# Sink keys in the own key block: query blocks of 112 in a fused attention and gated FFN kernel

## The chip, the cores and the metric

The kernel runs on one core of a Trainium2 chip. The metric is the device time of one execution in microseconds (us). The core has a matrix engine (TensorE, PE in the profile; its weight loads are shown apart as PEld), two engines for elementwise work (VectorE, DVE, and ScalarE, ACT), GpSimd (POOL), which here issues most of the loads, and SyncE (SP), whose queue carries a few loads, the transposing transfers and the stores. Matrix products accumulate in PSUM; everything else is held in the on-chip memory SBUF.

## The reference

What is computed is an attention with a sliding window and sinks, and then a feed-forward part without a nonlinearity. There are 4 batches, 8 heads, 768 tokens and 64 dimensions a head. A query sees the 128 keys up to and including its own, and the first 4 keys of the sequence, the sinks.

```python
scores = scale * np.matmul(q, k.transpose(0, 1, 3, 2))
rel = pos[:, None] - pos[None, :]
keep = (pos[None, :] < 4) | ((rel >= 0) & (rel < 128))
a = softmax(np.where(keep, scores, -1e9))
attn = np.matmul(a, v)
x = attn.transpose(0, 2, 1, 3).reshape(3072, 512)
out = ((x @ w1) * (x @ w2)) @ w3 @ w_out
```

w1 and w2 are 512 by 1024, w3 is 1024 by 1024, w_out is 1024 by 512. The output is 3072 by 512 in float32.

## The kernel before

**Folding.** The product w3 @ w_out does not depend on the tokens, so the kernel makes it once (`w3o`): TensorE transposes w3 in halves of a row block (`fold_w3`, tasks "t3", tile `w3t`, line 407) and multiplies pieces of it with w_out (`fold_mm`, "fm", tiles `ph` and `pw`, line 437). Each token then needs two gate products and one projection.

**Attention.** Keys and queries of a block of 128 tokens arrive as rows (`kN`, `qN`) and are turned into `kqT`, in which a head's 64 dimensions lie across partitions. For batches 0 and 1 TensorE does that (`transposes`, "tpk", tile `tp`, line 213), for batches 2 and 3 a transposing transfer on SP's queue ("tdk", "tdq", line 220). Values (`vN`) stay as they arrive, with a column of ones that gives the softmax its sum. Scores are made with keys across partitions (`scores`, "sc", line 260; batch 0's first blocks through `block_scores`, line 281): one call is for one pair of heads and one unit of 256 queries, two blocks, each with the block of keys before it and its own. ScalarE takes exponentials (`ex`), VectorE multiplies a 0/1 mask (`am`), and `values` ("av", line 350) loads each 128 by 128 piece of `am` as weights and streams the 65 columns of values and ones. VectorE divides by the sum (`rec`, `xn`).

**Sinks.** The 4 sink keys lie outside most windows. `sink_keys` ("sk", line 228) copies them into `ksbd`, which has 32 columns of weights for each pair of heads; `sink_scores` ("ss", tile `sp`, line 242) multiplies them with the queries after the first 256, for four pairs at once, and `es` is their exponential. `sink_values` ("sv", line 233) lays out the sink values (`vs`). In `values`, each block after the first unit starts with a product of `es` and `vs` that is 130 columns wide, both heads in one.

**FFN.** The normalized output is transposed to `xT`, by TensorE ("xt") for batch 0 and by transfers on SP's queue ("xd") for the others. `gate` ("g", line 390) makes one of the two gate products for 128 of the 1024 hidden columns and one stretch of tokens (`CHUNKS`): 3 x 256 tokens in batches 0 and 1, 2 x 384 in batches 2 and 3. ScalarE copies the first half (`a_sb`), VectorE multiplies the second with it into `ab`. `project` ("p", tile `po`, line 451) multiplies `ab` with `w3o`, and ScalarE (for one piece VectorE) copies the result out for a store.

**What sets the order.** Every step is a task. `plan()` simulates the engines with a table of costs, and picks at each moment the task that starts first and, among those, has the best priority; `nudge` shifts the priority of four tasks. The order so found is emitted, one in-order stream for each engine, so at run time an engine that waits for one operand holds everything behind it. PSUM holds four "mm" buffers for all but scores ("ph" apart) and two larger ones for scores. GpSimd's queue carries the loads in the order of the list `order`; an issue waits until the transfer eight places ahead of it has landed, since eight semaphores are in turn. The loads of batches 1 to 3 stand behind each other, a block's K, Q, V at a time (line 110).

Of the kernel before, what the change touches and what calls it, by code (L numbers as in the profile page):

```python
# [21 lines left out]
def kernel(  # L22
# [13 lines left out]
    nc = tc.nc  # L36
# [16 lines left out]
    CHUNKS = [[(256 * i, 256 * i + 256) for i in range(3)]] * 2 + [[(0, 384), (384, 768)]] * (B - 2)  # L53
    XPOSE = ((2, 0), (2, 1), (2, 2), (3, 0), (3, 1), (3, 2))
    BLOCKS = ((0, 0), (0, 1))
    SINKS = (1, 3)
# [15 lines left out]
    vc = const.tile([P, B, D], FP32, name="vc")  # L72
    maskt = const.tile([P, 2, 512], BF16, name="maskt")
# [5 lines left out]
    wo_sb = wp.tile([P, KFF, DM], BF16, name="wo_sb")  # L79
# [9 lines left out]
    vN = per_batch("vN", [P, NB, H, VS], 3)  # L89
# [5 lines left out]
    ksbd = per_batch("ksbd", [P, 648], 4)  # L95
    vs = per_batch("vs", [P, H, D + 1], 4)
    es = per_batch("es", [P, 512], 2)


    def rows(src, b, kb):  # L100
        return src[b, :, kb * P:(kb + 1) * P, :].rearrange("h p d -> p h d")
# [5 lines left out]

    def load_qkv(b, kb):
        for src, dst in zip(kqv, (heads(kN[b][:, kb, :]), heads(qN[b][:, kb, :]), vN[b][:, kb, :, 0:D])):
            nc.gpsimd.dma_start(out=dst, in_=rows(src, b, kb))  # L110
# [18 lines left out]
    def load(what, *i):  # L129
        if what == "qkv":  # L130
            if i[1] == 0:
                nc.gpsimd.memset(vN[i[0]][:, :, :, D:D + 1], 1.0)
            for kb in range(i[1], i[2]):
                load_qkv(i[0], kb)
        elif what == "w3":
# [3 lines left out]
        else:  # L139
            for dst, src in ((w1_sb, moe_w1), (w2_sb, moe_w2)):  # L140
# [8 lines left out]
    order = [("w3", 6, 8), ("qkv", 0, 0, 1), ("qkv", 0, 1, 2), ("w3", 5, 6), ("qkv", 0, 2, 3),  # L149
             ("qkv", 0, 3, 4), ("w12", 0, 1), ("w12", 1, 2), ("w12", 2, 3), ("w12", 3, 4), ("qkv", 0, 4, 5),  # L150
             ("qkv", 0, 5, 6), ("qkv", 1, 0, 6), ("qkv", 2, 0, 6), ("qkv", 3, 0, 6)]

    nudge = {("g", 0, 1, 5, 0): -300, ("g", 1, 0, 6, 1): 60, ("p", 3, 5, 256): -300, ("g", 2, 0, 3, 0): -300}
# [19 lines left out]
    idle = ksbd[B - 1]  # L173
    nc.vector.memset(idle[:], 0.0)
# [3 lines left out]
    for b in range(B - 1):  # L178
        nc.vector.memset(ksbd[b][:], 0.0)
# [4 lines left out]
    m4 = maskt[:].rearrange("p v (a c q) -> p (v a) c q", c=2, q=P)  # L184
    nc.gpsimd.affine_select(m4[:, :, 0, :], m4[:, :, 0, :], compare_op=ALU.is_ge, fill=0.0,
                            base=-1, pattern=[[0, 4], [-1, P]], channel_multiplier=1)
    nc.gpsimd.affine_select(m4[:, :, 1, :], m4[:, :, 1, :], compare_op=ALU.is_ge, fill=0.0,
                            base=0, pattern=[[0, 4], [1, P]], channel_multiplier=-1)
    nc.gpsimd.memset(maskt[0:4, 0, P:3 * P], 1.0)
# [7 lines left out]
    for b in range(B):  # L197
        nc.gpsimd.tensor_copy(vs[b][:, :, D], ones_s[:])
    for h in range(H):
        r0 = 32 * (h // 2) + 4 * (h % 2)  # L200
        nc.sync.dma_start(out=vc[r0:r0 + 4, :, :], in_=v[:, h, 0:4, :].rearrange("b s d -> s b d"))
    if hold:
        nc.gpsimd.tensor_copy(spent[:], casts[hold - 1][1][:, 0:1])
    for x in order:
        if x[0] != "qkv" or x[1] == 0:
            load(*x)

# [14 lines left out]

    def sink_keys(b):

        for e in range(2):
            hp = slice(64 * e, 64 * e + 64)
            kk = ksbd[b][hp, 4 * e:4 * e + 640].rearrange("p (r x) -> p r x", x=160)
# [3 lines left out]
    def sink_values(b):  # L231

        nc.vector.tensor_mul(vs[b][:, :, 0:D], vc[:, b:b + 1, :].to_broadcast([P, H, D]),
# [3 lines left out]
    def sink_scores(b, t0, t1):  # L237

        sp = ps_mm.tile([P, (t1 - t0) * 256], FP32, tag="mm", name="sp")
        for r in range(NP):  # L240
            rows = slice(32 * r, 32 * r + 32)
            nc.tensor.matmul(sp[rows, :], ksbd[b][:, r * P + 32 * r:r * P + 32 * r + 32],  # L242
                             qT[b][:, r, t0 * 256:t1 * 256], start=True, stop=True)
        yield
        nc.scalar.activation(es[b][:, (t0 - 1) * 256:(t1 - 1) * 256], sp[:], ACTF.Exp, scale=scale)
# [6 lines left out]
    ams = {}  # L252

# [210 lines left out]
    def keep_busy(n):  # L464

        pz = ps_mm.tile([P, 512], FP32, tag="mm", name="pz")
        for _ in range(n):
            nc.tensor.matmul(pz[:], idle[:, 0:P], idle[:, 0:512], start=True, stop=True)
# [362 lines left out]
```

## Time and profile before

| | |
|---|---|
| runs | 196.51, 196.13, 196.01 us; median 196.13 |
| profiled execution | span 193.9 us on the core, 4599 instructions |
| TensorE | 186.7 us busy (96%), 1808 products |
| VectorE, ScalarE, GpSimd | 114.7, 103.0, 75.2 us busy |
| gates and projection | 90.8 and 42.7 us of TensorE's busy time |
| attention values | 16.9 us in 296 products of 65 columns, 11.1 us in 56 of 130, by the time from start to end of each |
| DMA | 29.17 MB, 150 GB/s mean |

The time of a run is counted by the device; the profile shows the span of one profiled execution, from its first to its last instruction on the core, and has no second figure for that execution. The rows of the profile are read as follows. A row of the chain of waits is "start, duration, engine, output, line", with the count of instructions that were taken together. A row by stretch of time (a:b) gives its length, the busy time of the engine asked for with the count of instructions, the granted clock of TensorE, and the share and rate of DMA. A group of instructions is "busy time, mean ns of one | idle time before them, and what ended it". Products overlap in TensorE, so the mean of one (from start to end) is longer than what it adds to the sequence; the calls in the chain show the latter.

### The profile page before, as it was taken

How to read it: one execution, taken by the hardware profiler on the slowest of the kernel's cores; microseconds unless marked ns; L12 is line 12 of the kernel's file. 1: busy time of each engine (PE TensorE's matmuls, PEld its weight loads, DVE VectorE, ACT ScalarE, POOL GpSimd, SP SyncE). 2: the span in 40 equal slices, each digit the busy share in tenths (PEclk: the TensorE clock that was granted, in tenths of full speed). 3: DMA queues.
4: the chain of work that ended last, by engine and by line, in shares of the span. 5: the costliest groups of instructions: out<-in, count | busy, mean ns of one | idle time of the engine just before them, and what ended most of it. 6: DMA issues, size and time to landing. Idle time of an engine off the chain costs nothing.

```text
span 193.9 us, 4599 instructions
## 1 busy us (share of the span) xinstructions
PE 186.7 (96%) x1808; PEld 123.1 (63%) x1825; DVE 114.7 (59%) x277; ACT 103.0 (53%) x175; POOL 75.2 (39%) x102
## 2 busy tenths in 40 slices
PE   7899999999999999999999999999999999999994
PEld 2344556898867787588799556654666565655542
DVE  5554687856699887678785435660588564444100
ACT  4052289743766876575764627352884563333232
POOL 5189987688899863443155351000000000000000
PEclk9999999999999999999999999999999999999999
DMA  6999999999999999999999999999320432000144
GB/s 219 372 391 179 170 159 196 196 161 153 155 147 194 195 150 119 154 133 238 144 140 158 144 164 209 190 153 205 113 52 6 110 110 55 0 0 3 68 162 149
DMA packets 108021, 29.17 MB, mean 150 GB/s; under 512 B 98656, under 2 KB 103904, under 8 KB 108000
## 3 DMA queue, kind: packets, MB, share of 16 engines
q0 software_dynamic: 79520, 12.33, 90.4%
q1 hardware_dynamic: 28336, 16.49, 40.5%
q8 instruction: 14, 0.23, 0.5%
q10 hardware_dynamic: 144, 0.07, 0.1%
q14 instruction: 7, 0.06, 0.1%
HBM read 29.39 MB, written 6.29 MB: 184 GB/s over the span
## 4 chain that ended last, share of the span: by engine, by line
PE 88%; DMA 8%; SPq 1%; issue 1%; DVE 0%; POOL 0%; ACT 0%
PE pg L390 44%; PE po L451 21%; PE av L350 7%; PE sc L260 5%; DMA ab<-in_moe_w_out_dram 4%; DMA w_sb<-in_moe_w_dram 4%; PE tp L213 3%; PE pw L437 3%; PE av L313 1%; PE sc L281 1%; PE tp L407 1%; PE ph L437 1%; SPq L165 1%; PE sp L242 1%; PE xt L329 1%
## 5 line engine op out<-in xcount | busy, mean ns | idle before, releaser
L390 PE MATMUL pg<-xT,w_sb 128*128 128x256 bf16 (+1 forms) x640 | 90.8, 294 | 0.0
L390 PEld LDWEIGHTS <-w_sb 128*128 128x128 bf16 x640 | 59.8, 98 | 20.7 <-issue 1.7
L397 ACT COPY a_sb<-pg 128x256 f32<-128x256 f32 (+1 forms) x80 | 33.3, 416 | 37.4 <-PE pg L390 24.1
L394 DVE TENSOR_TENSOR ab<-a_sb,pg 128x256 bf16<-128x256 f32 (+1 forms) x80 | 37.6, 471 | 23.8 <-PE pg L390 21.2
L451 PE MATMUL po<-w3o,ab 128*128 128x512 bf16 (+2 forms) x196 | 42.7, 362 | 0.5
L265 ACT ACTIVATE ex<-sc 128x1024 bf16<-128x1024 f32 (+1 forms) x40 | 37.9, 963 | 5.3 <-PE sc L260 4.6
L269 DVE TENSOR_TENSOR am<-ex,maskt 128x1024 bf16<-128x1024 bf16 (+1 forms) x40 | 25.3, 646 | 12.8 <-ACT ex L265 12.8
L451 PEld LDWEIGHTS <-ab 128*128 128x128 bf16 x208 | 19.1, 98 | 19.7 <-issue 0.2
L455 ACT COPY w_sb<-po 128x512 f32<-128x512 f32 (+2 forms) x25 | 14.1, 564 | 26.2 <-PE po L451 24.1
L110 POOL DMA_DIRECT2D kN<-in_k_dram x24 | 21.6, 900 | 13.1 <-DMA qN<-in_q_dram 9.2
L110 POOL DMA_DIRECT2D qN<-in_q_dram x24 | 21.8, 909 | 11.9 <-DMA vN<-in_v_dram 7.7
L110 POOL DMA_DIRECT2D vN<-in_v_dram x24 | 21.4, 893 | 8.6 <-DMA kN<-in_k_dram 7.6
L357 DVE TENSOR_TENSOR xn<-av,rec 128x256 bf16<-128x256 f32 x40 | 17.0, 425 | 1.4
L350 PE MATMUL av<-vN,am 128*128 128x65 bf16 x296 | 16.9, 193 | 0.0
L350 PEld LDWEIGHTS <-am 128*128 128x128 bf16 x296 | 14.5, 97 | 2.3 <-issue 0.2
L354 DVE RECIPROCAL rec<-av 128x4 f32<-128x4 f32 x40 | 7.2, 180 | 12.3 <-PE av L350 12.2
L260 PE MATMUL sc<-kqT 64*128 64x128 bf16 (+1 forms) x216 | 11.6, 238 | 0.1
L350 PE MATMUL av<-vs,es 128*128 128x130 bf16 x56 | 11.1, 221 | 0.0
L285 ACT ACTIVATE ex<-sc 128x1024 bf16<-128x1024 f32 x7 | 7.1, 1045 | 5.3 <-PE sc L281 5.3
L260 PEld LDWEIGHTS <-kqT 64*128 64x128 bf16 x216 | 6.9, 94 | 4.0 <-issue 3.4
L215 DVE COPY kqT<-tp 128x1024 bf16<-128x1024 bf16 x12 | 8.3, 689 | 1.8 <-PE tp L213 1.7
L437 PE MATMUL ph<-wo_sb,w3t 128*128 128x512 bf16 x32 | 8.1, 379 | 0.4 <-DVE w3t L412 0.3
(70 smaller groups left out, 126.5 us busy)
## 6 DMA issues: line engine op xcount, KB each, us to landing
out_dram<-w_sb SPq DMA_DIRECT2D x20, 256.0 KB
kN<-in_k_dram POOLq DMA_DIRECT2D x24, 128.0 KB, 8.6
qN<-in_q_dram POOLq DMA_DIRECT2D x24, 128.0 KB, 8.2
vN<-in_v_dram POOLq DMA_DIRECT2D x24, 128.0 KB, 8.6
w_sb<-in_moe_w_dram POOLq DMA_DIRECT2D x9, 256.0 KB, 8.5
ab<-in_moe_w_dram SPq DMA_DIRECT2D x4, 512.0 KB
ab<-in_moe_w_out_dram SPq DMA_DIRECT2D x2, 512.0 KB
out_dram<-w_sb SPq DMA_DIRECT2D x7, 128.0 KB
```

Of the source, the lines that this page charges most:

```text
L110: nc.gpsimd.dma_start(out=dst, in_=rows(src, b, kb))
L260: nc.tensor.matmul(sc[:, e, c:c + n], kT[b][hp, r, kb * P:(kb + 1) * P], qT[b][hp, r, qb * P:qb * P + n], start=True, stop=True)
L265: nc.scalar.activation(ex[:, :, c0:], sc[:, :, c0:], ACTF.Exp, scale=scale)
L269: nc.vector.tensor_mul(am[:, :, c0:], ex[:, :, c0:], mk)
L350: nc.tensor.matmul(o, lhs, rhs, start=(n == 0), stop=(n == len(todo) - 1), skip_group_check=True)
L357: nc.vector.tensor_mul(xns[b, t][:, :, r, :, :], av[:, :, :, 0:D], rec[:].to_broadcast([P, 2, 2, D]))
L390: nc.tensor.matmul(pg[:], w_sb[:, kk, dt * P:(dt + 1) * P], xT[b][:, kk, tk], start=(kk == 0), stop=(kk == NP - 1))
L394: nc.vector.tensor_mul(ab[b][:, dt, tk], gate_a.pop((b, c, dt))[:], pg[:])
L397: nc.scalar.copy(a_sb[:], pg[:])
L437: nc.tensor.matmul(po, w3T[i][:, j, :], wo_sb[:, j, :], start=(j == 0), stop=(j == KFF - 1))
L451: nc.tensor.matmul(po[:], ab[b][:, kk, m * P:(m + 1) * P], w3o[:, kk, n0:n1], start=(kk == 0), stop=(kk == KFF - 1))
L455: (nc.vector.tensor_copy if n0 == DM // 2 else nc.scalar.copy)(o_sb, po[:])
```

## The change

It touches batches 1 to 3 alone (`LATE`); batch 0 keeps the separate sinks.

Query blocks no longer have 128 tokens each. They are cut at 0, 128, 256, 320, 432, 544, 656 and 768 (`CUTS`), and make up three units of 320, 224 and 224 queries (`UNITS`). From the third block on, a block of 64 or 112 queries has an own key block (`kown`) that begins with the 4 sink keys and goes on with the block's 64 or 112 keys. VectorE copies these (`own_keys`, "ko"). The score product against that block gives the sinks' scores too, in rows 0 to 3, and the mask leaves them in. `vN` has 7 slots cut in the same way, whose first 4 rows from the third slot on hold the sink values. So no sink keys, scores, exponentials or values are made apart in these batches.

The 128 keys before a block of 112 lie in `kqT` as they did. Their values straddle two slots of `vN`, so they are put together in a new tile `vp` by transfers from SBUF to SBUF (`before_slot`, "vk"): one that spreads the sink values over the slots, four for the second unit and two for the third, 7 a batch, on GpSimd's queue among the loads. The third V block of a batch comes in two loads, since a cut goes through it. `vp` of batches 1 and 3 lies where w_out was; most of the transposed pieces of w3 lie in `kown` while the fold lasts.

A value product of the second and third unit now has 112 columns of weights in place of 128, and there are 8 for a pair of heads and a unit; the first unit, of three blocks, has 10.

Gate stretches follow the units: 320, 224, 224 in batch 1, and 320, 448 in batches 2 and 3. The transposing transfers for `xT` are 7 a batch for 6.

TensorE's order is no longer chosen: `pe_pick` takes the next task of a written list, `TURNS`, with all tasks of the kernel in it, and the cost table only sets the order on the other engines, shifted by a second table (`LEAN`) for 44 steps. `nudge` is empty.

```diff
-    CHUNKS = [[(256 * i, 256 * i + 256) for i in range(3)]] * 2 + [[(0, 384), (384, 768)]] * (B - 2)
+    SINK = 4
+    LATE = range(1, B)
+    CUTS = (0, 128, 256, 320, 432, 544, 656, 768)
+    QB = list(zip(CUTS, CUTS[1:]))
+    UNITS = ((0, 1, 2), (3, 4), (5, 6))
+    SPANS = [(QB[u[0]][0], QB[u[-1]][1]) for u in UNITS]
+
+    CHUNKS = [[(256 * i, 256 * i + 256) for i in range(3)], SPANS] + [[SPANS[0], (SPANS[1][0], S)]] * (B - 2)
...
-    wo_sb = wp.tile([P, KFF, DM], BF16, name="wo_sb")
+    wo_sb = inp.tile([P, KFF, DM], BF16, tag="wo", bufs=1, name="wo_sb")
...
+    vp = [None] + [inp.tile([P, 4, H, VS], BF16, tag=("wo", "vp")[1 - b % 2], bufs=1, name=f"vp_{b}") for b in LATE]
+    kown = [None] + [inp.tile([P, NP, 5, P], BF16, tag=f"kown{b % 2}", bufs=1, name=f"kown_{b}") for b in LATE]
...
+    def before_slot(b, part):
+
+        x, o = vN[b], vp[b]
+        if part == 0:
+            if b < 3:
+                clear_own(nc.gpsimd, b)
+            moves = [(x[0:SINK, 2:7], x[0:SINK, 0:1].to_broadcast([SINK, 5, H, VS]))]
+        elif part == 1:
+            moves = [(o[0:64, 0], x[64:P, 1]), (o[64:P, 0], x[SINK:SINK + 64, 2]),
+                     (o[0:16, 1], x[SINK + 48:SINK + 64, 2]), (o[16:P, 1], x[SINK:SINK + 112, 3])]
+        else:
+            moves = [(o[0:16, 2:4], x[SINK + 96:SINK + 112, 3:5]), (o[16:P, 2:4], x[SINK:SINK + 112, 4:6])]
+        for dst, src in moves:
+            nc.gpsimd.dma_start(out=dst, in_=src)
...
-             ("qkv", 0, 5, 6), ("qkv", 1, 0, 6), ("qkv", 2, 0, 6), ("qkv", 3, 0, 6)]
-
-    nudge = {("g", 0, 1, 5, 0): -300, ("g", 1, 0, 6, 1): 60, ("p", 3, 5, 256): -300, ("g", 2, 0, 3, 0): -300}
+             ("qkv", 1, 0, 6), ("vk", 1, 0), ("qkv", 2, 0, 2), ("vk", 1, 1), ("vk", 1, 2), ("qkv", 2, 2, 4),
+             ("vk", 2, 0), ("qkv", 2, 4, 6), ("vk", 2, 1), ("qkv", 3, 0, 2), ("vk", 2, 2), ("qkv", 3, 2, 4),
+             ("vk", 3, 0), ("qkv", 3, 4, 6), ("vk", 3, 1), ("vk", 3, 2)]
+
+    nudge = {}
...
+    def own_keys(b, u):
+
+        if u < 0:
+            if b == 3:
+                clear_own(nc.vector, b)
+            nc.vector.tensor_copy(kown[b][:, :, :, 0:SINK],
+                                  kT[b][:, :, 0:SINK].rearrange("p r (o x) -> p r o x", o=1)
+                                  .to_broadcast([P, NP, 5, SINK]))
+        elif u == 0:
+            nc.vector.tensor_copy(kown[b][:, :, 0, SINK:SINK + 64], kT[b][:, :, QB[2][0]:QB[2][1]])
+        else:
+            t0, t1 = SPANS[u]
+            nc.vector.tensor_copy(kown[b][:, :, 2 * u - 1:2 * u + 1, SINK:SINK + 112],
+                                  kT[b][:, :, t0:t1].rearrange("p r (m x) -> p r m x", m=2))
+        yield
...
+    def late_scores(b, r, u):
+
+        if u == 0:
+            todo = [(64, kT[b][:, r, 0:P], 0, 2 * P), (64 + 2 * P, kT[b][:, r, P:2 * P], P, P + 64),
+                    (0, kown[b][:, r, 0, :], 2 * P, 64)]
+            n = 512
+        else:
+            todo, n = [], 448
+            for i, s in enumerate(UNITS[u]):
+                q0 = QB[s][0]
+                todo += [(224 * i, kT[b][:, r, q0 - P:q0], q0, 112), (224 * i + 112, kown[b][:, r, s - 2, :], q0, 112)]
...
+    def late_values(b, r, u):
...
+            def add(i, k1, c, m, s):
+                src = vN[b][0:k1, s, h, 0:D + 1] if s >= 0 else vp[b][0:k1, -1 - s, h, 0:D + 1]
+                todo.append((av[0:m, i, e, :], am[0:k1, e, c:c + m], src))
+
+            if u == 0:
+                add(0, P, 64, P, 0)
+                add(1, P, 64 + P, P, 0)
+                add(1, P, 64 + 2 * P, P, 1)
+                add(2, 64 + SINK, 0, P, 2)
+                add(2, P, 448, 64, 1)
+            else:
+                for i, s in enumerate(UNITS[u]):
+                    add(i, P, 224 * i, 112, 2 - s)
+                    add(i, 112 + SINK, 224 * i + 112, 112, s)
...
+    TURNS = [("t3", 0, 0), ("t3", 2, 0), ("t3", 0, 1), ("t3", 4, 0), ("t3", 2, 1), ("fm", 0, 0), ("fm", 2, 0), ("fm", 4, 0),
...
+    LEAN = {(("sc", 0, 0, 0), 2): -1, (("sc", 0, 3, 1), 2): 1, (("sc", 0, 0, 2), 2): -0.4, (("sc", 0, 3, 2), 1): -2.5,
...
+            if len(line) == len(TURNS):
+                return None
+            k = tasks[TURNS[len(line)]]
+            assert all(a in begun for a in k["started"]), k["name"]
```

Two places in the instruction streams show what moves. The number behind a tile's name is that of its buffer: `vN_92`, `qN_84` and `kN_88` are batch 1's, `vN_93`, `qN_85` and `kN_89` batch 2's, `vp_107` is batch 1's. A row's waits name the semaphores that it waits for; DMASW0 to 7 are those of GpSimd's transfers in turn.

GpSimd, from batch 1's last V load to batch 2's third block, before:

```order
L110 DMA vN_92<-in_v_dram 128x8x64 [waits DMASW5_49]
L132 MEMSET vN_93 128x48
L110 DMA kN_89<-in_k_dram 128x8x64 [waits DMASW6_49,PE_49]
L110 DMA qN_85<-in_q_dram 128x8x64 [waits DMASW7_49,PE_49]
L110 DMA vN_93<-in_v_dram 128x8x64 [waits DMASW0_49]
L110 DMA kN_89<-in_k_dram 128x8x64 [waits DMASW1_49]
L110 DMA qN_85<-in_q_dram 128x8x64 [waits DMASW2_49]
L110 DMA vN_93<-in_v_dram 128x8x64 [waits DMASW3_49]
L110 DMA kN_89<-in_k_dram 128x8x64 [waits DMASW4_49]
```

The same place after, from batch 2's second V load on:

```order
L124 DMA vN_93<-in_v_dram 128x8x64 [waits DMASW5_49]
L144 DMA vp_107<-vN_92 64x576 [waits DMASW6_49]
L144 DMA vp_107<-vN_92 64x576 [waits DMASW7_49]
L144 DMA vp_107<-vN_92 16x576 [waits DMASW0_49]
L144 DMA vp_107<-vN_92 112x576 [waits DMASW1_49]
L144 DMA vp_107<-vN_92 16x1152 [waits DMASW2_49]
L144 DMA vp_107<-vN_92 112x1152 [waits DMASW3_49]
L120 DMA kN_89<-in_k_dram 128x8x64 [waits DMASW4_49]
```

Between batch 2's second and third block there are now the six copies into `vp_107`, each with a turn of the eight semaphores; the copy that spreads the sink values stands ahead of batch 2's first K load.

TensorE, a value call of batch 1's second unit (`es_116` and `vs_112` are its sink scores and values), before:

```order
L350 MATMUL av<-vs_112,es_116 128x130 [waits Activation_49]
L350 LDWEIGHTS am
L350 MATMUL av<-vN_92,am 128x65
L350 LDWEIGHTS am
L350 MATMUL av<-vN_92,am 128x65
```

And after, the first value call of that unit:

```order
L518 MATMUL pg<-xT_99,w_sb 128x256
L370 LDWEIGHTS am [waits DMASW7_49,DMASW6_49]
L370 MATMUL av<-vp_107,am 112x65 [waits DVE_49]
L370 LDWEIGHTS am
L370 MATMUL av<-vN_92,am 112x65 [waits DMASW5_49]
L370 LDWEIGHTS am [waits DMASW1_49]
L370 MATMUL av<-vp_107,am 112x65 [waits DMASW0_49]
```

The sink product at the head of a block has gone, the products have 112 rows of output, and the call waits for the four copies into `vp_107`; the gate product ahead of it belongs to batch 0, and more of these follow the call.

More of the change, by code (lines that the diff above doesn't have):

```diff
@@ L252 @@
     ams = {}
+    def late_scores(b, r, u):
[8 more added lines that the diff above has]
+                todo += [(224 * i, kT[b][:, r, q0 - P:q0], q0, 112), (224 * i + 112, kown[b][:, r, s - 2, :], q0, 112)]
+        sc = ps_sc.tile([P, 2, 512], FP32, tag="sc", name="sc")
+        for c, keys, q0, m in todo:
+            for e in range(2):
+                hp = slice(64 * e, 64 * e + 64)
+                nc.tensor.matmul(sc[:, e, c:c + m], keys[hp], qT[b][hp, r, q0:q0 + m], start=True, stop=True)
+        yield
+        ex = work.tile([P, 2, 512], BF16, tag="ex", name="ex")
+        nc.scalar.activation(ex[:, :, 0:n], sc[:, :, 0:n], ACTF.Exp, scale=scale)
+        yield
+        am = work.tile([P, 2, 512], BF16, tag="am", bufs=4, name="am")
+        mv = 2 * min(u, 1)
+        nc.vector.tensor_mul(am[:, :, 0:n], ex[:, :, 0:n], maskt[:, mv:mv + 1, 0:n].to_broadcast([P, 2, n]))
+        ams[b, r, u] = am
+        yield
@@ L497, in landings @@
                     issue = max(issue, landed[len(ready) - 8])
+                what = queues["pool"][len(ready)][3][0]
+                if what[0] == "vk":
+                    needs = [("v", what[1], s) for s in ((0,), (1, 2, 3), (3, 4, 5))[what[2]]]
+                    if any(x not in arrive for x in needs):
+                        break
+                    issue = max([issue] + [arrive[x] + 0.3 for x in needs])
                 issue += queues["pool"][len(ready)][0]
@@ L562 @@
     last_av = []
+    late = []
     for b in range(B):
@@ L615 @@
                 after = list(qk)
-                if b >= 2 and t == 0:
-                    after += [("g", b - 2, len(CHUNKS[b - 2]) - 1, dt, 1) for dt in range(KFF)]
                 lead = r % 2 == 0
@@ L680, in plan @@
         queue = {"act": [], "dve": [], "sp": []}
+        line = []
         def spare(ring):
```

257 lines of the change are left out of this document (153 added, 104 removed), and 63 rows, old and new, of tables (LEAN, TURNS, order).

## The prediction, on record before the changed kernel was run

> **What bounds the kernel now.** The page came first: the span, the share of each engine, the slices, the chain that ended last.
>
> ```profile
> span 193.9 us, 4599 instructions
> PE 186.7 (96%) x1808; PEld 123.1 (63%) x1825; DVE 114.7 (59%) x277; ACT 103.0 (53%) x175; POOL 75.2 (39%) x102
> PEclk9999999999999999999999999999999999999999
> DMA  6999999999999999999999999999320432000144
> PE 88%; DMA 8%; SPq 1%; issue 1%; DVE 0%; POOL 0%; ACT 0%
> ```
>
> TensorE is busy for 96% of the span at full granted clock, and 88% of the chain is its work. The DMA engines are full until slice 28 (some 136 us), so a transfer that is added before then delays others. The chain in order of time and TensorE's busy time by stretch tell where the chain is not TensorE's:
>
> ```profile
> 10.47 0.38 POOL spent L203
> 10.85 7.31 DMA w_sb<-in_moe_w_dram
> 18.21 0.40 PE tp L407 x4
> ...
> 188.65 2.36 PE po L451 x20
> 191.03 0.27 ACT w_sb L455
> ```
> ```profile
> 20.20:41.00 20.80, 20.21 (x261) 1.00 1.84 180
> sum 172.80, PE 171.47; mean PE 28.58
> ```
>
> Up to 18.2 us the chain is loads. From there to 191.0 it is TensorE, which is idle for 1.3 of 172.8 us, 0.6 of them between 20.2 and 41. So two sums matter: what TensorE has to do after its first loads, and what it comes to wait for in the new order. The profiled execution spans 193.9 us and the runs' median is 196.13; I carry the 2.2 us between them over unchanged.
>
> **The products.** From the chain, for whole calls:
>
> ```profile
> 60.48 0.45 PE tp L213 x8
> ...
> 64.78 0.33 PE sp L242 x4
> 81.24 0.72 PE av L350 x20
> 82.39 0.44 PE sc L260 x8
> 85.12 0.18 PE av L350 x6
> 92.87 0.22 PE sp L242 x4
> 102.45 5.24 PE pg L390 x48
> 107.69 0.55 PE sc L260 x12
> ```
>
> Sink scores of batches 1 to 3 go: one call over 512 queries in batches 1 and 3 (0.33 each), two over 256 in batch 2 (0.22 each): **-1.10 us**.
> Values: a pair of heads costs 0.18 for the first 256 queries and 0.36 for each of the other two parts (0.72 for two calls), 0.90 in all. After, it is 10, 8 and 8 products of 65 columns without the 130-wide sink products. At 0.18/6 = 30 ns each these 26 cost 0.78. Twelve pairs: **-1.44 us**.
> Scores: a pair of heads streams 384+512+512 = 1408 columns before and 512+448+448 = 1408 after, in 22 products for 16. Two calls with 12 products differ from two with 8 by 0.11 us, and 256 more columns at 5.24/(48x256) = 0.426 ns make the same 0.11; four more products cost nothing there. I take 0.
> Gates keep their 640 products and their columns (320/224/224 or 320/448 in place of thirds or halves of 768): 0.
> Together **-2.54 us** of TensorE work, if a value product still costs 30 ns.
>
> **Its weight load** is the open price: 192 value products now load 112 columns of masked scores and 24 load 64, where every value product loaded 128.
>
> ```profile
> L350 PEld LDWEIGHTS <-am 128*128 128x128 bf16 x296 | 14.5, 97 | 2.3 <-issue 0.2 <-DVE rec L354 0.2
> L242 PEld LDWEIGHTS <-ksbd 128*32 128x32 bf16 x24 | 0.6, 92 | 1.3 <-issue 1.3
> ```
>
> A load of 128 columns takes 97 ns and one of 32 takes 92, so 112 should lie between. These are times from start to end; the products follow each other every 30 ns, so loads overlap, and the rows do not say what a shorter one does to that pace. Lower bound 0. Upper bound: no overlap, 97 ns a product, (97-30) x 192 = +12.9 us. I take 0, by the 92 and 97.
> The Trainium skill speaks against that ("TensorE: Matmul & The Clock Gate", section "Weight-path perf modes — Fast Weight Load (FWL) and DoubleRow"): the fast load is on when the number of weights is 128 and the type is not FP32. Its section "LDWEIGHTS (loading the stationary operand)" puts a load at columns/1.2 ns, 93 for 112, an estimate of +12 us here; the trace contradicts that formula for 32 columns (27 by it, 92 measured), and no run here shows 112. What the rule would do is the first rival.
>
> **The start.** The first Q block gates its transposes:
>
> ```profile
> L110 POOL DMA_DIRECT2D qN<-in_q_dram x1: 893/893/893, 12.7 to 12.7; - x1
> DMA to landing us min/median/max: 7.5/7.5/7.5
> ```
> ```profile
> 20.24 0.40 PE L213 MATMUL tp<-ident,qN 128*128 128x128 bf16 x4
> ```
> ```profile
> 18.61 0.43 PE pw L437 x2
> 19.47 0.22 PE tp L407 x4
> ```
>
> Issued at 12.7, it lands at 20.2, and the transposes follow at once. The change moves nothing ahead of this load on POOL that matters: POOL waits until 10.47 (the first row of the chain above) for a raw weight in both. Before, 12 half transpositions of w3 and 17 pieces of the fold stand ahead of that point; in the written list 11 and 15. That is 0.22 + 2 x 0.43 = 1.08 us less done by a moment that does not move. It has to be done later, and between 20.2 and 41 only 0.6 us of idle time could take it up (loads there end waits too). I take **+1.0 us** (bounds 0.5 and 1.1).
>
> **The copies.** Keys before a block of 112 straddle two slots of vN, so their values are copied by DMA into vp. The four copies of batch 1's second unit stand on POOL's queue behind batch 2's second V block.
>
> ```profile
> L110 POOL DMA_DIRECT2D vN<-in_v_dram x1: 972/972/972, 62.2 to 62.2; - x1
> DMA to landing us min/median/max: 8.8/8.8/8.8
> ```
> ```profile
> 68.57 0.46 PE av L350 x10
> 66.16 0.88 POOL L110 DMA_DIRECT2D kN<-in_k_dram  x1 [0.38 <-DMA qN<-in_q_dram]
> ```
>
> ```profile
> L110 POOL DMA_DIRECT2D kN<-in_k_dram x1: 987/987/987, 63.0 to 63.0; - x1
> DMA to landing us min/median/max: 9.5/9.5/9.5
> ```
>
> That V block lands at 62.2 + 8.8 = 71.0, the K block issued next at 63.0 + 9.5 = 72.5. The last of the four copies waits for the slot of batch 2's first Q block, whose landing releases the issue at 66.16; so it enters the queue at about 66, behind the V block. Before, TensorE starts these values at 68.57. In the list more is ahead of them: four gate halves (+1.75, at 0.44), four value calls of 10 products for 6 (+0.48), the wider scores of the first unit (+0.22), less one block transposition (0.45), one sink call (0.33) and about 0.1 of other scores: 1.55 us, and the 1.08 that the start left over. So it comes there at about 71.2. TensorE is strictly in order: behind these values wait gate halves whose inputs are ready. Lower bound 0 (the copies land with the V block); upper 1.4 (they land with the K block, at 72.5). I take **+0.6 us**.
>
> **The rest.** VectorE gets a third block to normalize in the first unit, copies of own keys, and loses two kinds of sink work:
>
> ```profile
> 60.00:80.00 20.00, 17.25 (x46) 1.00 2.09 159
> ```
> ```profile
> L357 DVE TENSOR_TENSOR xn<-av,rec 128x256 bf16<-128x256 f32 x40 | 17.0, 425 | 1.4
> L215 DVE COPY kqT<-tp 128x1024 bf16<-128x1024 bf16 x12 | 8.3, 689 | 1.8 <-PE tp L213 1.7
> L233 DVE TENSOR_TENSOR vs<-vc,ones_s 128x512 bf16<-128x512 f32 x4 | 2.7, 687 | 0.6 <-DMA vc<-in_v_dram 0.6
> L228 DVE COPY ksbd<-kqT 64x16 bf16<-64x16 bf16 x8 | 1.3, 163 | 0.1
> ```
>
> Four wider normalizations a batch add at most 4 x 0.21, the two large key copies at most 0.69 each and the two small ones 0.16 to 0.3; against them go 0.69 + 2 x 0.16: about +1.6 us a batch. In the tightest stretch that is 18.9 of 20 us, hidden behind TensorE; with that cover gone it would cost at most the 1.6. ScalarE loses the four sink exponentials. Both: 0.
>
> Sum: -2.54 + 1.0 + 0.6 = -0.9 us: span 193.0, median **195.2 us**. A measurement here tells about 0.3% (0.6 us) from no change.
>
> **Rivals.**
> 1. *The 112-column loads set the pace of the value products.* Place: the second and third unit of batches 1 to 3. If such a load advances one column per beat, as a streamed product does, it takes 112 x 0.426 = 48 ns and no longer fits under the 30: +18 ns x 192 = +3.4 us, **198.6**. For it: no row has a load of 112. Against it: 92 beside 97 ns. From 5 ns more a product on, the gain is gone. By the Trainium skill's rule named above this is the case to expect; the trace can't decide it.
> 2. *Transfers are late.* 21 copies and 3 more V loads on a queue that is full, and 3 more DMA transposes on SP. The first unit of a batch covers 320 queries and needs the third K and Q block transposed as well:
>
> ```profile
> 72.08 1.50 SPq L220 DMA_TRANSPOSE kqT<-qN  x1
> 76.31 1.52 SPq L220 DMA_TRANSPOSE kqT<-qN  x1
> ```
> Before, batch 2's first scores (82.39 above) come 10.3 us after the issue at 72.08 of the last transposition they need. The third block's is issued at 76.31, so its scores are safe from 86.6. The list brings TensorE there later than 82.4, by nine gate halves of 320 columns (320 x 4 x 0.426 = 0.54 each, 4.9), less the sink call (0.33) and the values' saving (0.48), and by the start's 1.08: 5.2 us, and 0.6 at the copies, so 88.2. A delay of the queue decides from 1.6 us on. Each load there paces 1.6 us, so two loads' pace is 3.2 and leaves a wait of 1.6 at these scores. With the copies at 1.4 for 0.6, TensorE's lateness takes 0.8 of that back: about +1.6 to the sum in all, 196.8, **197** as priced. For it: DMA full. Against it: the copies are small, and the loads keep their order.
> 3. *The start costs nothing and the copies are in time:* 196.1 - 2.5 = **193.6**. For it: later order may be denser. Against it: 0.6 us of idle time is all there is to use.
>
> **How the numbers follow.** Forecast (193.9 to 196.2) 0.53; rival 1 0.23; rival 2 0.15; rival 3 0.09. Faster than 195.5: 0.41 of the forecast and all of rival 3, **0.50**. Within 0.6 of 196.1: 0.12 of the forecast, 0.06 of rival 2, 0.02 of rival 1, **0.20**. Slower: 0.21 of rival 1 and 0.09 of rival 2, **0.30**. The forecast's own range, 193.9 to 196.2, grows to **193.4 to 198.9** so as to hold rival 1 at 48 ns, rival 2 and most of rival 3; a full 97 ns is left out.
>
> **What would show it.** In the new profile: value calls of 8 products at 0.24 us in the chain (0.38 means rival 1); no sink scores past batch 0; TensorE idle for about 1 us or more before the first transposes and for 0.6 at the first products from vp near 71 us; no wait over 0.3 at batch 2's first scores. A value product over 35 ns, or idle time of TensorE over 3 us between 41 and 160, would make the prediction wrong.

## The result

The changed kernel takes **205.02 us** (median of 6 runs, 204.8 to 205.79), the kernel before 196.26 beside it. The ratio is 1.0446, 95% interval 1.0405 to 1.0488: 8.8 us slower, where 0.9 us less was forecast. The time lies above the stated range. Executions in a slower state of the chip, which some of the kernels below had, are left out of all medians and ratios.

The page of the changed kernel: span, shares, granted clock, the chain by engine.

```profile
span 203.3 us, 4779 instructions
PE 196.1 (96%) x1885; PEld 130.1 (64%) x1885; DVE 118.6 (58%) x280; ACT 101.9 (50%) x171; POOL 91.7 (45%) x134
PEclk9999999999999999999999999999999999999999
PE 86%; DMA 7%; POOL 3%; SPq 1%; issue 1%; ACT 0%
```

TensorE is still busy for 96% and still at full clock; it is busy for 9.4 us more (196.1 for 186.7), and the span grew by 9.4. So it is TensorE's own work that takes longer; new waits are small beside it. The chain of waits of the changed kernel (start, duration, what) names it. The first value call is of batch 1's first unit, the second of its second:

```profile
57.66 0.36 POOL kown L128
...
64.97 0.65 PE av L370 x10
65.62 0.55 PE pg L518 x4
66.16 0.65 PE av L370 x10
...
73.90 0.39 PE av L370 x8
74.29 1.78 PE pg L518 x16
```

A call of 10 products takes 0.65 us where the prediction counted 0.30, a call of 8 takes 0.39 for 0.24. The timeline of TensorE shows the second kind product by product (start, duration, instruction with weights, operands):

```profile
73.82 0.22 PE L370 MATMUL av<-vp,am 128*112 128x65 bf16 x1
73.87 0.22 PE L370 MATMUL av<-vN,am 116*112 116x65 bf16 x1
73.92 0.22 PE L370 MATMUL av<-vp,am 128*112 128x65 bf16 x1
```

The starts are 52 ns apart (the rows round to 10 ns), for 30 before; the first product of the call still takes 30, so 30 + 7 x 52 = 394 ns. It makes no difference whether the values lie in vp or vN, or the keys in 128 or 116 rows. The groups of weight loads by shape (busy, mean ns of one) show the other side:

```profile
L370 PEld LDWEIGHTS <-am 128*112 128x112 bf16 x96 | 10.8, 130 | 1.3
L370 PEld LDWEIGHTS <-am 128*128 128x128 bf16 x72 | 4.3, 99 | 1.6
L370 PEld LDWEIGHTS <-am 128*64 128x64 bf16 x24 | 2.5, 106 | 1.3
```

A load of 112 columns takes longer (130 ns) than one of 128 (99). Where the time goes, in the terms of the prediction:

| term | predicted | measured |
|---|---|---|
| products left out (sinks 1.10, values 1.44 at 30 ns) | -2.54 | -2.54 if the products were at 30 ns |
| 24 calls of 8 with 112 columns: 24 x (0.39 - 0.24) | 0 | +3.7 |
| 12 calls of 10 with two products of 64 columns: 12 x (0.65 - 0.30) | not seen | +4.2 |
| the gate or projection behind 10 of these calls (0.55 for 0.44, as at 65.62) | not seen | +1.1 |
| start: 1.08 us of the fold left for later, less a wait of 0.4 that only the kernel before has | +1.0 | +0.7 |
| copies into vp late | +0.6 | 0 |
| own key block cleared late on GpSimd | not seen | +0.6 |
| sum | -0.9 | +7.8 |

The last waits are in TensorE's list of waits (who waited for whom: us, times, longest):

```profile
PE sc L335 <- POOL kown L128: 0.6, 1, 0.6
PE tp L263 <- DMA qN<-in_q_dram: 0.6, 1, 0.6
PE tp L263 <- DMA kN<-in_k_dram: 0.2, 1, 0.2
```

The first is the late clear. The other two, 0.8 us together, are at the start: by the first Q transposition, which begins at 20.26 us for 20.24 before, TensorE has done 1.08 us less of the fold, as forecast. The kernel before then waits where the changed one does not:

```profile
22.09 0.40 PE L281 MATMUL sc<-kqT 64*128 64x128 bf16 x8 [0.37 <-DVE kqT L215]
```

The table is made from the two profiled executions, whose spans differ by 9.4 us, so it lacks 1.6. (The times differ by only 8.8: the profiled execution of the changed kernel took 204.98 us, 1.7 more than its span, where the prediction carried over 2.2. So the profiled execution of the kernel before was probably some 0.5 us faster than its median.) Of these, 0.6 us lies behind TensorE's last product. The last copy out of PSUM ends 2.6 us before the end of the span in the kernel before (191.03 + 0.27 of 193.9) and 3.2 in the changed one, of 203.3:

```profile
199.81 0.27 ACT w_sb L583
```

Why the end takes longer stays open, and for the remaining 1.0 us no cause is known.

### The profile page after: what moved, and what is told of

Same layout as the page of the kernel before. It is cut to its first block, busy times and chain, and to the rows that moved or that the text cites. A ratio compares the mean times of both kernels' runs of the same rounds, so it can differ in the third digit from the quotient of the medians.

```text
span 203.3 us, 4779 instructions
## 1 busy us (share of the span) xinstructions
PE 196.1 (96%) x1885; PEld 130.1 (64%) x1885; DVE 118.6 (58%) x280; ACT 101.9 (50%) x171; POOL 91.7 (45%) x134
## 4 chain that ended last, share of the span: by engine, by line
PE 86%; DMA 7%; POOL 3%; SPq 1%; issue 1%; ACT 0%
PE pg L518 41%; PE po L579 21%; PE av L370 9%; PE sc L335 5%; DMA ab<-in_moe_w_out_dram 4%; DMA qN<-in_q_dram 4%; PE pw L565 3%; PE tp L263 2%; PE av L441 1%; PE sc L408 1%; POOL qN L120 1%; PE ph L565 1%; POOL kN L120 1%; SPq L203 1%; PE tp L535 1%
## 5 line engine op out<-in xcount | busy, mean ns | idle before, releaser
L518 PE MATMUL pg<-xT,w_sb 128*128 128x256 bf16 (+3 forms) x640 | 92.0, 294 | 0.0
L522 DVE TENSOR_TENSOR ab<-a_sb,pg 128x256 bf16<-128x256 f32 (+3 forms) x80 | 37.5, 473 | 33.0 <-PE pg L518 32.2
L525 ACT COPY a_sb<-pg 128x256 f32<-128x256 f32 (+3 forms) x80 | 33.0, 415 | 43.4 <-PE pg L518 39.2
L338 ACT ACTIVATE ex<-sc 128x896 bf16<-128x896 f32 (+1 forms) x36 | 33.1, 954 | 5.3 <-PE sc L335 5.0
L583 ACT COPY w_sb<-po 128x512 f32<-128x512 f32 (+2 forms) x25 | 14.1, 564 | 28.7 <-PE po L579 27.4
L120 POOL DMA_DIRECT2D kN<-in_k_dram x24 | 22.1, 921 | 12.9 <-DMA vN<-in_v_dram 5.5
L342 DVE TENSOR_TENSOR am<-ex,maskt 128x896 bf16<-128x896 bf16 (+1 forms) x36 | 22.7, 641 | 2.5 <-ACT ex L338 2.5
L370 PEld LDWEIGHTS <-am 128*128 128x128 bf16 (+2 forms) x312 | 19.9, 118 | 4.6
L370 PE MATMUL av<-vN,am 116*112 116x65 bf16 (+3 forms) x216 | 21.8, 207 | 0.0
L377 DVE TENSOR_TENSOR xn<-av,rec 112x256 bf16<-112x256 f32 (+1 forms) x36 | 16.9, 469 | 1.2
L370 PE MATMUL av<-vp,am 128*112 128x65 bf16 x96 | 11.9, 215 | 0.0
L335 PE MATMUL sc<-kqT 64*128 64x112 bf16 (+2 forms) x144 | 10.0, 228 | 0.0
```

Source lines behind the costliest of these rows:

```text
L120: nc.gpsimd.dma_start(out=heads(dst[b][:, kb, :]), in_=rows(src, b, kb * P, (kb + 1) * P))
L335: nc.tensor.matmul(sc[:, e, c:c + m], keys[hp], qT[b][hp, r, q0:q0 + m], start=True, stop=True)
L338: nc.scalar.activation(ex[:, :, 0:n], sc[:, :, 0:n], ACTF.Exp, scale=scale)
L342: nc.vector.tensor_mul(am[:, :, 0:n], ex[:, :, 0:n], maskt[:, mv:mv + 1, 0:n].to_broadcast([P, 2, n]))
L370: nc.tensor.matmul(o, lhs, rhs, start=(x == 0), stop=(x == len(todo) - 1), skip_group_check=True)
L377: nc.vector.tensor_mul(xns[b, u][0:m, 0:n, r, :, :], av[0:m, :, :, 0:D], rec[0:m, 0:n].to_broadcast([m, n, 2, D]))
```

## The experiments

**The two kinds of loads, apart and together.** Three kernels widen the value products to 128 columns of weights. For the second and third unit the segments are exchanged, so that behind each 112 columns there are others:

```diff
-                todo += [(224 * i, kT[b][:, r, q0 - P:q0], q0, 112), (224 * i + 112, kown[b][:, r, s - 2, :], q0, 112)]
+                c = 224 * (1 - i)
+                todo += [(c, kT[b][:, r, q0 - P:q0], q0, 112), (c + 112, kown[b][:, r, s - 2, :], q0, 112 if i else P)]
...
-                    add(i, P, 224 * i, 112, 2 - s)
-                    add(i, 112 + SINK, 224 * i + 112, 112, s)
+                    add(i, P, 224 * (1 - i), P, 2 - s)
+                    add(i, 112 + SINK, 224 * (1 - i) + 112, P, s)
```

> Edit: in the changed kernel the value products of the second and third unit load 128 columns of masked scores in place of 112 (the extra 16 are a neighbour's scores and go to output rows that nothing reads; to have them, one own block a unit streams 128 queries for 112). Theory 'columns' (a load of 112 columns sets the pace): such a product goes from 52 ns to 30 ns, a call of 8 from 0.39 to about 0.24 us, 192 x 22 ns = 4.2 us less: about 200.8 us. Rival 'operands' (the 116 rows of keys, or values that lie in vp, slow them): nothing changes, 205.0 us, calls stay at 0.39.

For the first unit the segments, and the mask with them, stand in another order:

```diff
-                add(2, 64 + SINK, 0, P, 2)
-                add(2, P, 448, 64, 1)
+                add(2, 64 + SINK, P + 64, P, 2)
+                add(2, P, P, P, 1)
```

> Edit: in the changed kernel's first unit the 24 value products that load 64 columns load 128 (the scores' segments lie in another order, so that the 64 columns behind are there; the extra output rows are not read). The products of 112 columns stay. Theory 'change of form' (each change between a load of 128 columns and one of 64 costs 106 to 118 ns, in both directions): a call of 10 goes from 0.65 to 0.30 us, and the operation behind it loses about 0.1 more: 12 x 0.35 = 4.2 to 12 x 0.45 = 5.4 us less, 199.6 to 200.8 us. Rival 'rows' (the products over 68 rows of keys cause it): no change, 205.0 us.

> Edit: both paddings together; every value product loads 128 columns as in the kernel before. Theory: the two costs are apart and add up, 205.0 - 4.2 - 4.2 to 5.4 = 195.4 to 196.6 us, so about the kernel before, with a span of 193.8 to 195.0; TensorE still waits for the clear of kown at 57 us and for the first Q block at 20 us. The prediction's own sum, 195.2, would be met with both waits. Rival 'order' (the written list or the transfers cost several us by themselves): 198 us or more.

The first gave a ratio of 1.0354 (1.0294 to 1.0414; median 202.35), the second 1.0285 (1.0226 to 1.0344; 201.54). The chains of waits, of the first and of the second:

```profile
73.53 0.26 PE av L371 x8
```
```profile
97.07 0.31 PE av L371 x10
```

Both theories of the columns hold, and both rivals fall: the 116 and 68 rows of keys and the values in vp are still there. Of the first, 0.39 - 0.26 = 0.13 for 24 calls is 3.1 us, less than the 4.2 expected: the first product of a call cost 30 ns already, and a product takes 31 to 32 ns and not 30. By the ratios, from the changed kernel's 1.0446, the times fell by 1.8 and 3.2 us, each known to 1 to 1.5 us. The profiled execution of the first spans 200.2 us, 3.1 less than the changed kernel's 203.3, about as its products say. In the second, two waits take back a part:

```profile
PE sc L335 <- POOL kown L128: 1.2, 1, 1.2
PE sc L335 <- DMA kqT<-qN: 0.9, 1, 0.9
```

With both paddings the six executions lay between 198.16 and 206.63, too far apart for a ratio. The same kernel was run again:

> The same kernel as the run with both paddings, whose six times lay between 198.2 and 206.6 us, for a second profile. Theory 'late transfers decide': TensorE's products cost as little as there (values 13.9 us in all), and in every execution TensorE waits for transposed keys near 102 and 148 us, by 1 us or more in all; times of 198 to 203 us, spread by when the loads land. Rival 'a disturbed execution': without the disturbance these waits are under 0.5 us in all and the time is 195.5 to 197 us.

Now 200.01 (198.95 to 200.74), ratio **1.0196** (1.0134 to 1.0258). The value products are at 31 to 32 ns, and the kernel is still 3.8 us slower than before. What holds it then is in part in the profile of this run, in VectorE's timeline and TensorE's (in brackets the idle time ahead, and whose end it was put down to):

```profile
149.79 0.40 DVE L285 COPY kown<-kqT 128x896 bf16<-128x896 bf16 x1 [2.96 <-DMA kqT<-kN]
150.10 0.61 DVE L524 TENSOR_TENSOR ab<-a_sb,pg 128x448 bf16<-128x448 f32 x1
```
```profile
150.77 0.19 PE L372 MATMUL av<-vp,am 128*128 128x65 bf16 x1 [1.62 <-DVE ab L524]
```

VectorE stands for 2.96 us before batch 3's copy of own keys, which waits for a transposed key block. Behind it in VectorE's order is a gate multiplication whose inputs were ready; it holds a PSUM buffer, and TensorE waits 1.62 us. The theory is that the transposition is late because the loads are. TensorE's wait is 1.6 us in this execution; how much of the 3.8 us comes from late loads, the next run tells.

**The copies.** Both paddings, without the copies into vp:

```diff
-        for dst, src in moves:
+        for dst, src in moves if part == 0 else ():
             nc.gpsimd.dma_start(out=dst, in_=src)
...
-                    add(i, P, 224 * (1 - i), P, 2 - s)
+                    add(i, SINK + (64 if s == 3 else 112), 224 * (1 - i), P, s - 1)
```

> The changed kernel with both paddings and without the 18 copies into vp: the value products of the window before a block read the slot before it (so these values are wrong; the number of products and columns stays). Theory 'the copies' bytes delay the loads' (18 copies move 1.8 MB on a DMA that moves about 150 GB/s in all): batch 3's last V load lands at about 134 us in place of 145 to 150, the transposes of its keys come in time, TensorE has no wait over 0.5 us after 60 us, and the time is 195.4 us (as the sum says, with the two waits at 20 and 57 us). Rival 'the written list': the waits of 1.4 to 2.2 us at 102 and 148 us stay, 198 to 202 us.

196.9 us, ratio 1.0048 (1.0017 to 1.0079). The same copy on VectorE in this run:

```profile
146.27 0.39 DVE L285 COPY kown<-kqT 128x896 bf16<-128x896 bf16 x1
```

No wait ahead of it, and 3.5 us sooner. So with fast products the copies cost 1.0196 - 1.0048 = 1.5%, about 2.9 us (the two intervals lie apart), by the transfers that they delay. The last V load lands at 123.85 + 14.1 = 138.0, 2.5 us earlier than with copies and not at 134; the theory holds in kind, its size for that load not.

The same without the paddings:

```diff
-                    add(i, P, 224 * i, 112, 2 - s)
+                    add(i, SINK + (64 if s == 3 else 112), 224 * i, 112, s - 1)
```

> The changed kernel, no padding, without the 18 copies into vp (these values are wrong, the products stay). With fast loads the copies cost 201.8 - 196.9 = 4.9 us. Theory 'hidden by the slow products': here TensorE comes some 8 us later to batch 3's scores, its waits past 60 us were 0, so the time stays within 0.3% of 205.0. Rival 'copies cost either way': 1 us or more less, 204 us or under.

205.41 us, ratio 1.0435 (1.038 to 1.049): nothing, as the theory has it. In the changed kernel the slow products bring TensorE to each place so late that the late transfers are hidden behind it. The two costs do not add up: take the larger away, and the smaller appears.

**How the cost depends on the columns.** The kernel before, with the value products cut to other widths:

```diff
+        cut = CUT.get((b, t, r), P)
         for n, (o, lhs, rhs) in enumerate(todo):
+            if cut < P and rhs.shape[-1] == D + 1:
+                o, lhs = o[0:cut], lhs[:, 0:cut]
```

> The kernel before, in which the value products of the second and third unit of batches 1 to 3 load only the first m of their 128 columns of scores, with another m for each pair of heads: 127, 124, 120, 112 in batch 1, 104, 96, 80, 72 in batch 2, 68, 64, 48, 32 in batch 3; the sink products keep 128. It leaves out the window's part for the last 128 - m queries of each block there. Theory 'a column a beat': each product under 128 columns takes about m x 0.43 ns + 4 (57 ns at 124, 52 at 112, 45 at 96, 35 at 72), so the pace falls with m; at 64 and fewer it is 30 ns again, but each of the changes to and from a sink product costs 105 to 120 ns more. Rival 'fixed penalty': every m under 128 takes the same 52 ns. With the first, the 192 products of 65 to 127 columns and more (9 sizes x 16 products) cost about 1.4 to 2.5 us in all and the three sizes of 64 and fewer 3 x 4 x 0.22 = 2.7 us: some 200 us.

200.31 us in one execution, as expected. The groups of weight loads by shape, with the mean of one behind the comma:

```profile
L355 PEld LDWEIGHTS <-am 128*128 128x128 bf16 x104 | 5.1, 97 | 1.2 <-DVE rec L359 0.2 <-issue 0.2
L355 PEld LDWEIGHTS <-am 128*127 128x127 bf16 x16 | 1.2, 140 | 0.1
L355 PEld LDWEIGHTS <-am 128*112 128x112 bf16 x16 | 1.1, 131 | 0.0
L355 PEld LDWEIGHTS <-am 128*96 128x96 bf16 x16 | 1.0, 124 | 0.0
L355 PEld LDWEIGHTS <-am 128*72 128x72 bf16 x16 | 0.9, 115 | 0.1
L355 PEld LDWEIGHTS <-am 128*64 128x64 bf16 x16 | 0.8, 109 | 0.6 <-issue 0.5
L355 PEld LDWEIGHTS <-am 128*32 128x32 bf16 x16 | 0.7, 96 | 0.6 <-DVE xn L362 0.2 <-issue 0.2
```

From 32 to 127 columns a load grows by 0.46 ns a column ((140 - 96)/95). 128 lies on no such line: it is as short as 32. The distance from one value product to the next, from the ends of the products in the trace, is 59 ns at 127 columns, 57 at 124, 52 at 112, 45 at 96, 35 at 72, 32 at 64, and 30 at 128. So the theory of a column a beat holds, with about 4 ns on top; a fixed penalty does not. The first product behind a sink product takes 30 to 32 ns at any width over 64, which fits a load that goes on beside the 56 ns of that 130-wide product.

At 64 columns and fewer there is another cost. Here are calls with 68 and with 64 columns in TensorE's timeline:

```profile
144.33 0.22 PE L355 MATMUL av<-vs,es 128*128 128x130 bf16 x1
144.39 0.29 PE L355 MATMUL av<-vN,am 128*68 128x65 bf16 x4
144.52 0.22 PE L355 MATMUL av<-vs,es 128*128 128x130 bf16 x1
...
147.31 0.22 PE L355 MATMUL av<-vs,es 128*128 128x130 bf16 x1
147.46 0.31 PE L355 MATMUL av<-vN,am 128*64 128x65 bf16 x4
147.70 0.23 PE L355 MATMUL av<-vs,es 128*128 128x130 bf16 x1
```

From one sink product to the next it is 0.19 us with 68 columns and 0.39 with 64. The first product of 64 comes 0.15 us after the sink product, for 0.06 with 68, and the way back costs as much again. To see whether the change costs or the load, the changed kernel's two products of 64 were put side by side:

```diff
+        if u == 0:
+            todo = todo[0:4] + todo[5:9] + [todo[4], todo[9]]
```

> Edit: in the changed kernel's first unit the two products of 64 columns in a call stand next to each other at its end, so that a call has one stretch of 64-column loads in place of two. Nothing else changes. Theory 'change of form' (the change costs, not the load): 12 x (0.118 + 0.106) = 2.7 us less, 202.3 us; the second product of 64 columns takes about 30 ns. Rival 'each load of 64 is slow': the second one still takes 148 ns, only the way back to 128 columns is saved once, 12 x 0.106 = 1.3 us, 203.7 us.

202.6 us, ratio 1.0356 (1.0307 to 1.0405). In the chain of waits:

```profile
64.55 0.43 PE av L372 x10
```

0.65 - 0.43 = 0.22 a call, the whole of 0.118 + 0.106, and in the trace the second product of 64 takes 31 ns. The change of form is what costs; the time alone would not tell the theory's 202.3 us from the rival's 203.7.

**The two waits.**

```diff
-            if b < 3:
+            if b == 2:
                 clear_own(nc.gpsimd, b)
...
-            if b == 3:
+            if b != 2:
                 clear_own(nc.vector, b)
...
-             ("fm", 3, 0), ("t3", 6, 0), ("tpk", 0, 0), ("fm", 1, 3), ("fm", 3, 1), ("t3", 7, 0), ("t3", 7, 1), ("fm", 3, 2),
+             ("fm", 3, 0), ("t3", 6, 0), ("fm", 1, 3), ("fm", 3, 1), ("t3", 7, 0), ("tpk", 0, 0), ("t3", 7, 1), ("fm", 3, 2),
```

> The changed kernel, no padding, with its two waits taken away: batch 1's own key block is cleared by VectorE in place of GpSimd, and three tasks of the fold (two pieces, half a transposition, 1.08 us) come ahead of the first transposition of batch 0. Theory 'two waits': TensorE's 0.57 us ahead of the first Q transposition and 0.60 at the first own-key scores at 57 us go, about 1.2 us, 205.0 to 203.8. Rival 'moved waits': the first scores of batch 1 then wait for the clear on VectorE or for the key copy, and no more than the start's part is won: 204.5 or the same.

204.63 us, ratio 1.0391 (1.033 to 1.0453). The interval overlaps the changed kernel's, so a gain of 1.2 us is neither shown nor excluded by the time. TensorE's waits and VectorE's timeline of this run:

```profile
PE tp L535 <- DVE kown L540: 1.0, 1, 1.0
```
```profile
20.71 0.69 DVE L299 TENSOR_TENSOR vs<-vc,ones_s 128x512 bf16<-128x512 f32 x1 [2.53 <-DMA vc<-in_v_dram]
```

The wait for the clear is gone. The start's wait has moved: a transposition of w3 now waits 1.0 us for a PSUM buffer, whose copy stands on VectorE behind the sink values, which wait 2.53 us for a small transfer. So at the start the wait moved, as the rival has it.

With both paddings, no copies and these two edits:

> Both paddings, no copies into vp (these values are wrong), and the two waits taken away as in the run of the changed kernel of this call: the change without any cost that the prediction's sum of products does not hold. That sum is -2.54 us against the kernel before. Theory: the products do save what the sum says, so 196.9 - 1.2 = 195.7 or less, at or under the kernel before (195.8 to 196.1), by 0.4 to 2.5 us. Rival 'the saving is smaller': products of 65 columns over 68 and 116 rows take 31 to 32 ns and the list leaves 0.3 us elsewhere, so that it is the same as before within 0.3%.

196.15 us, ratio **1.0001** (0.9957 to 1.0044). Even with every cost that the runs named taken away, this kernel does not save 2.54 us; it saves at most 0.8 (0.0043 of 196). The padding has a price of its own in it: one own block of a unit streams 128 queries for 112, which is 12 pairs x 2 units x 2 heads x 16 columns at 0.426 ns, some 0.3 us by this estimate.

An attempt at a better version, with both paddings and all copies, with the same two edits and a planner that counts on later key transpositions:

```diff
-                    done[k["name"]] = at + (9.2 if at < end - 4.0 else 6.0 if at < end else 3.0)
+                    done[k["name"]] = at + (12.5 if k["name"][0] == "tdk" and at > 80.0 and at < end - 4.0 else 9.2 if at < end - 4.0 else 6.0 if at < end else 3.0)
```

> The changed kernel with both paddings, all copies in place, and three changes of order: batch 1's own key block is cleared by VectorE and not by GpSimd behind the loads; the first transposition of batch 0 comes three tasks of the fold later; and the planner counts 12.5 us in place of 9.2 for a transposing transfer of keys in the loaded stretch, so that VectorE's copies of own keys stand later in its order. Theory 'in-order VectorE behind a late own-key copy': the 2.2 us at 102 us go, and about 0.6 + 0.6 at 20 and 57 us; batch 3's keys are as late as before, so a wait of 1 to 3 us stays at 148 us: 195 to 198 us. Rival 'loads late': waits only move, 198 to 202 us.

202.0 and 201.16 us, ratio 1.0289 (1.019 to 1.0388), for the paddings alone 1.0196 (1.0134 to 1.0258): not better, and the intervals overlap, so worse is not shown either. The profiled execution took 204.2 us, longer than the two of the ratio, and its chain of waits shows what held this one:

```profile
97.87 2.79 SPq L507
100.75 6.83 DMA kqT<-qN
107.63 0.95 PE sc L336 x16
```

A Q transposition stands on SP's in-order queue behind transposes of x that come later, and TensorE waits for it until 107.6. No version beat the kernel before.

## Why the prediction was wrong, point by point

**What bounds the kernel** was right: TensorE's own work, at 96% in both.

**The weight load is the step that failed.** It said "A load of 128 columns takes 97 ns and one of 32 takes 92, so 112 should lie between", and "I take 0, by the 92 and 97". Between two widths a third was read off a straight line, but the two are not on one line: from 32 to 127 columns the load grows, and 128 is a case of its own. The value products measured 0.39 and 0.65 us a call in place of 0.24 and 0.30: 9.0 us with what stands behind the calls, for the 0 that was taken. The upper bound of the step, 12.9, held it; the range did not, as it ended at rival 1.

**Rival 1** had the mechanism and nearly the size: 48 ns a product and +3.4 us forecast, 52 ns and +3.7 measured. The price, one column a beat, came from the streamed products (0.426 ns a column) and holds. Its place was too narrow: it left out the 24 products of 64 columns in the first unit, which cost 5.3 us of the 9.0, by the change of form. That price stood in a row that the prediction quoted: `64.78 0.33 PE sp L242 x4` is four products of 32 columns of weights side by side that stream 512 columns, which is 512 x 0.426 = 0.22 us. The other 0.11 was not asked about; it is about what the sweep gives for a change to 32 columns (133 ns for the first product, in place of 30).

The Trainium skill's page "TensorE: Matmul & The Clock Gate", section "Weight-path perf modes — Fast Weight Load (FWL) and DoubleRow", has the rule that the prediction weighed and set aside: the fast load is there at 128 weights. The trace agrees, 97 ns at 128 and 140 at 127. The Trainium skill's formula on the same page, in "LDWEIGHTS (loading the stationary operand)", columns/1.2 ns, would be 93 ns at 112; the distance measured is 52, so that the measurement decides. The Trainium skill's page "TensorEngine Tiling (Array Packing)", section "Key Properties", says that a change of the tiling mode drains TensorE, and its section "Available Configurations" has modes of 64 and 32 columns; the 0.10 to 0.12 us at each change to 64 and back agrees, and the prediction did not draw on it. That a load of 64 columns or fewer among loads of 128 is such a change of mode is inferred, not shown.

**The products.** Sinks: as forecast, no sink scores past batch 0. Values: at 128 columns they take 31 to 32 ns, close to the 30 that was counted. But the sum of -2.54 was never seen whole: in the run without any named cost the kernel is level with before. Half a microsecond is the 31 to 32 ns (312 products), 0.3 us is the padding's own price, and 0.6 us is the longer end behind TensorE's last product, which every kernel with the change has. In the profiled execution TensorE also waits 0.7 us for a Q transposition and 0.4 that are put down to ScalarE's exponentials. These come to about the 2.5 us, but that execution took 197.0 us and the median is 196.15, so that the account is not closed.

**The start**: +1.0 forecast, about 0.7 measured, and the working was right: 1.08 us of the fold is left over, and a wait takes up a part. Moving three tasks does not simply win it back, as the run shows that did so.

**The copies**: +0.6 forecast, 0 measured. They landed in time since TensorE came to them at 73.9 and not at 71.2: the last of the four is issued at 65.94 and lands 6.3 us later, at 72.2. What was forecast there is true of the kernel with fast products, at another place: not TensorE's wait for vp, but VectorE's for keys. **Rival 2** priced late transfers at 1.6 us; they are worth about 2.9, and only where rival 1 does not come first. The two were treated as separate cases, and one hides the other.

**The rest**: VectorE and ScalarE were hidden, as said. GpSimd's clear of the own key block was not costed at all: it stands behind batch 1's loads on an in-order queue, and the first scores with own keys wait 0.6 us for it.

## What to carry to other kernels

A duration from start to end does not give the pace of overlapping instructions, and two sizes do not give a third: before a tile size is changed, the new size needs a row or an experiment of its own, and where no row has it, its rival's price belongs into the range for every place that uses it. Where the streamed side is as narrow as these 65 columns (28 ns at 0.426 ns each), keep weights at 128 columns even if the extra ones are thrown away, and do not alternate between 128 and 64 or fewer. And where one engine is so late that it hides others' lateness, a cost measured as 0 is 0 only until that engine is made faster.

## What the runs showed of the hardware that was not expected

A bf16 weight load of 127 columns sets a pace of 59 ns for products that stream 65 columns, one of 128 at most 30 to 32: one column less nearly doubles the time. Going from weights of 128 columns to 64 or fewer costs 100 to 120 ns, and so does the way back; between products of the same form it is 31 ns.

After a long stop of TensorE its granted clock was lower. These are single executions, so this is seen and not explained, and nothing above rests on it. TensorE's busy time and granted clock (the figure behind the count of instructions) around a stop of 4.6 us in the last attempt, around one of 2.2 us in the first run with both paddings, and around one of 1.6 us in the second:

```profile
103.00:107.60 4.60, 0.07 (x3) 1.00 1.88 157
107.60:110.00 2.40, 2.37 (x25) 0.52 1.64 195
110.00:112.50 2.50, 2.50 (x31) 0.78 1.65 119
```
```profile
102.00:104.30 2.30, 0.13 (x2) 0.95 1.86 87
104.30:107.00 2.70, 2.70 (x33) 0.50 2.07 166
```
```profile
149.20:150.80 1.60, 0.03 (x2) 1.00 1.04 208
150.80:152.00 1.20, 1.20 (x14) 1.00 0.00 1
```

After 4.6 us the clock is at 0.52 and 0.78 in the two stretches that follow (an estimate of the cost: 2.4 x 0.48 + 2.5 x 0.22 = 1.7 us), after 2.2 us at 0.50, and after 1.6 us it stays at 1.00.
